# Cached attention on one core: when a load may be issued

## The chip, the cores and the metric

The kernel runs on one core of one Trainium2 chip. The metric is the device time of one execution in microseconds (us), lower is better. The profile is one execution, recorded by the hardware profiler; its span goes from the first to the last instruction.

## The reference

Two independent blocks A and B of multi-head attention with a key/value cache, each followed by an output projection; the results stand side by side in the output. All tensors are bf16, `B, Sq, D = 16, 64, 640`, `H, Sk, Dh = 32, 512, 128`.

```
def _A_ref(x, k_cache, v_cache, wq, wo):
    q = (x @ wq).reshape(B, Sq, H, Dh).transpose(0, 2, 1, 3)
    scores = jnp.einsum("bhqd,bhkd->bhqk", q, k_cache) * (Dh ** -0.5)
    p = softmax(scores, axis=-1)
    o = jnp.einsum("bhqk,bhkd->bhqd", p, v_cache)
    return o.transpose(0, 2, 1, 3).reshape(B, Sq, H * Dh) @ wo
return jnp.concatenate([A(...), B(...)], axis=-1)
```

Each block reads 2 x 67 MB of keys and values, which are used once.

## The kernel before

The work is cut into four passes (two blocks, each in two halves of 16 heads). A pass goes over 8 pairs of batches, and a pair over its 16 heads, one head of both batches at a time. Two heads make one step `m` (256 steps), and two steps make a chunk of four heads (128 chunks).

For each step TensorE transposes the keys (`em_KX`, L586), multiplies them with the queries (`em_SM`, L632), transposes the probabilities (`em_TR2`, L670), multiplies them with the values (`em_PV2`, L694), and adds the heads' outputs times `wo` (`em_OP2` and `em_OX`, L709 and L719). The projection of the queries (`em_Q`, L603) is spread between these. VectorE copies the transposed keys (L593), takes the row maxima (L641) and the reciprocals; ScalarE computes the exponentials (L647); GpSimd scales the rows (L661).

The order of every engine's instructions is fixed when the program is built: `PHASES` gives each kind of operation an offset in steps and a place in a period, `build_plan` sorts by the resulting planned time `ts`, and `prune_waits` leaves of all dependences only the semaphore waits that are not implied by others. On TensorE a wait is attached to a matmul; where an operation needs more waits than its first instruction and the last one of the operation before it can carry, a separate waiting instruction stands ahead of it.

All loads are issued by SyncE (its rows in the profile say SPq), in one order, sorted by a key: the planned time of the first use less `LEAD` or `WLEAD` steps, or, if that is later, the planned time at which the buffer comes free. A step needs one load of keys (`LDK`, 512 KB, `kn_ring`, 9 buffers) and one of values (`LDV`, 512 KB; `v_ring` has 5 buffers, each of two halves with a load of its own, and a chunk needs both halves). Loads of 640 KB bring 16 slices each of `wq` and `wo`; `x` comes in three loads (block A) and eight of 160 KB (block B, `xr_ring`). SyncE issues in program order, so a load that waits holds all loads behind it.

When a load may be issued is what the change touches. Before, the plan holds a model of TensorE's time (`STEP_US`), of the time that each load takes (`DMA_US`) and a time before which no load is counted (`START_US`). For each load it takes the modelled time `t_now`, but at the latest `BEFORE` (3.88) steps ahead of the first use, finds the TensorE operation planned for that time, and makes the load wait for it (`paced`). This comes on top of the wait for a free buffer. Both halves of a `v_ring` buffer count on one semaphore; the waiting instruction waits for both.

Of the kernel before, what the change touches and what calls it, by code (L numbers as in the profile page):

```python
# [15 lines left out]
class Cfg:  # L16
# [5 lines left out]
    NVP = 5  # L22
    LEAD = 5.37
    WLEAD = 5.48
    STEP_US = ((8, 3.68), (32, 27.17), (160, 3.12), (216, 3.1), (256, 3.43))
    DMA_US = dict(LDK=1.40, LDV=1.44, LDWQ=1.8, LDWO=1.8, LDX=0.45, LDXR=0.5)
    START_US = 210.96
    BEFORE = 3.88
    NKT = 3
    NXR = 2  # L30
    NP = 4
# [108 lines left out]
def build_plan(dims, cfg):  # L140
# [17 lines left out]
    KT = dims["KT"]  # L158
# [5 lines left out]
    progs = {e: [] for e in ENGINES}  # L164
# [21 lines left out]
    for k in range(NPER - PPQ):  # L186
        u, i, hc = k // PPQ, k % PPQ // HG, k % HG
# [20 lines left out]
    def x_of(k):  # L208
        u, b = (k - HG) // PPQ + 2, (k - HG) % PPQ // HG
        if k % HG or u < 4 or u >= NPER // PPQ or u % 4 > 1:  # L210
            return None
        return u // 4, u % 2 * QB + b
# [102 lines left out]
    for n, (k_lo, *templates) in enumerate(cfg.PHASES):  # L315
        k_hi = cfg.PHASES[n + 1][0] if n + 1 < len(cfg.PHASES) else 0
        for eng, template in zip(("pe", "act", "dve", "pool"), templates):
            for kind, off, sub, t in template:
                for m in range(2 * (k_lo % NPER) + off % 2, 2 * (k_hi % NPER or NPER), 2):
                    op = make_op(kind, m, sub, m - off + 2 * t / cfg.PERIOD)  # L320
# [11 lines left out]
    loads = []  # L332
# [5 lines left out]
    for ps_ in range(NPASS):  # L338
        for j in range(HG):
            ready = []  # L340
            if ps_:
                first = ("QN", (2 * ps_ - 1) * MPQ + j * MPG, 0)
                ready = [("QN", (2 * ps_ - 2) * MPQ + j * MPG + MPG - 2, 0)]
            else:
                first = ("QZ", 2 * j - 2, 0 if j > 1 else G) if j else ("QJ", 0, 0)
            add(ready, first, cfg.WLEAD, 0, "LDWQ", (ps_, j), [("wq", qslot(j))], (ps_, j))
            i = ps_ * HG + j
# [8 lines left out]
    for n, m in enumerate(xts):  # L356
        xb, b = x_of(m // 2)
# [8 lines left out]
            [("v", k % cfg.NVP, j)], m)  # L366


    def us(t):
        us_, a = min(t, 0) * cfg.STEP_US[0][1], 0  # L370
        for b, step in cfg.STEP_US:
            us_ += step * max(0, min(t, b) - a)
            a = b
        return us_

    pe_us = [us(op.ts) for op in progs["pe"]]
    paced = []
    t_now = cfg.START_US
    for key, first, _, op in sorted(loads, key=lambda e: e[:3]):
        t_now = max(t_now, us(key))  # L380
        i = bisect.bisect_right(pe_us, min(t_now, us(first - cfg.BEFORE))) - 1
        if i > 0:
            paced.append((op, progs["pe"][i]))
        progs["sp"].append(op)
        t_now += cfg.DMA_US[op.kind] * (op.aux[2] - op.aux[1] if op.kind == "LDX" else 1)

    counts = {}

    def sem_key(op):
        if op.kind in ("LDK", "LDV", "LDXR"):  # L390
            return ("d_" + op.kind[2:].lower(), op.writes[0][1])
        if op.kind == "LDX":
            return ("d_x", op.aux[1])
        if op.kind in ("LDWQ", "LDWO"):
            return ("d_" + op.kind[2:].lower(), op.writes[0][1])
        if op.kind == "ST":
            return ("d_out",)
        if op.kind in ("INIT1", "INIT2"):
            return ("s_init",)
        return ("s_" + op.kind.lower(),)  # L400

    def assign(op):
        key = sem_key(op)
        counts[key] = counts.get(key, 0) + 1
        op.sem = key
        op.count = counts[key]
# [11 lines left out]
    for op in sorted(all_ops, key=lambda o: (o.ts, ENGINES.index(o.eng))):  # L418
# [6 lines left out]
        for res in op.writes:  # L425
# [3 lines left out]
            for rd in readers.get(res, ()):  # L429
                if rd is not op:  # L430
# [2 lines left out]
            readers[res] = []  # L433
        op.deps = [d for d in deps if d is not op and not (d.eng == op.eng and op.eng in ("pe", "sp"))
                   and not (d.dma and op.dma and d.eng == op.eng)]
    for op, d in paced:
        op.deps.append(d)
    info = dict(NSTEP=NSTEP, NMAC=NMAC, NCHUNK=NCHUNK, NGRP=NGRP, HG=HG, NBP=NBP, SPB=SPB, NHALF=NHALF,
                NPASS=NPASS, counts=counts, KT=KT, wslot=wslot, qslot=qslot, QB=QB, PPQ=PPQ, qcell=qcell,
# [63 lines left out]
def mha_kernel(nc, blocks, out, cfg=None):  # L503
# [12 lines left out]
    N1 = DN - N0  # L516

    progs, info = build_plan(dict(NBLK=NBLK, B=B, H=H, KT=KT), cfg)
    prune_waits(progs)
    NBP, SPB, NHALF = info["NBP"], info["SPB"], info["NHALF"]  # L520
# [413 lines left out]
```

## Time and profile before

| | |
|---|---|
| median of 3 runs | 852.0 us (849.78 to 853.32) |
| the profiled execution: its own time | 852.97 us |
| its span | 851.0 us |
| mean granted TensorE clock | 0.998 |
| TensorE busy (matmul) | 811.3 us, 95% |
| VectorE, ScalarE, GpSimd busy | 727.9, 644.7, 417.1 us |
| read from HBM | 292.03 MB, of it 292.06 MB on SyncE's queue (by packets) |

The profile's page lists busy time by engine, the span in 40 slices, the DMA queues, the chain of work that ended last, groups of instructions by source line, and the DMA issues with their median time from issue to landing. "PEld" is TensorE's loading of weights. A row such as "PE ps L603 <- issue: 18.0, 113, 0.2" says that TensorE sat idle ahead of line 603 for 18.0 us in total, 113 times, at most 0.2 us, and that nothing which the profile shows was waited for. Queue q1 carries SyncE's loads, q10 the stores of the output (issued by ScalarE), q8 and q14 the engines' instructions.

### The profile page before, as it was taken

The numbers are of one execution on the slowest core, as the hardware profiler recorded it, in microseconds if no ns is written. First come the engines' busy times: TensorE is split into PE (matmuls) and PEld (weight loads), VectorE is DVE, ScalarE is ACT, GpSimd is POOL, SyncE is SP. The second block draws the span as 40 slices with busy tenths as digits, with TensorE's granted clock in tenths as the row PEclk, the third lists the DMA queues.
The fourth block names the chain that finished last, engine by engine and source line by source line (L and its number), as shares of the span: only waits on it lengthen the run. The fifth ranks groups of instructions, "written<-read, shape, count | busy, mean of one in ns | idle before, by whom it ended". The sixth has DMA issues, their size and how long they took to land.

```text
span 851.0 us, 38366 instructions
## 1 busy us (share of the span) xinstructions
PE 811.3 (95%) x17025; PEld 566.4 (67%) x17156; DVE 727.9 (86%) x1192; ACT 644.7 (76%) x1466; POOL 417.1 (49%) x518
## 2 busy tenths in 40 slices
PE   8999999999999999999999998999999999999996
PEld 5566676666666666666666666666666666666664
DVE  4688888888888898888899887988888989989994
ACT  2678877777777787777877877787887877778886
POOL 0355455454544554454554545455455455455553
PEclk9999999999999999999999999999999999999999
DMA  9999999999999999999999999999999999999992
GB/s 306 360 354 349 369 354 352 348 338 362 354 352 353 369 369 363 359 360 367 364 362 367 364 360 349 321 362 362 360 360 363 366 369 365 366 339 352 370 321 89
DMA packets 228438, 297.14 MB, mean 349 GB/s; under 512 B 9136, under 2 KB 162736, under 8 KB 228272
## 3 DMA queue, kind: packets, MB, share of 16 engines
q1 hardware_dynamic: 225968, 292.06, 100.3%
q8 instruction: 134, 2.20, 1.1%
q10 hardware_dynamic: 2304, 2.62, 0.9%
q14 instruction: 32, 0.26, 0.1%
HBM read 292.03 MB, written 2.62 MB: 346 GB/s over the span
## 4 chain that ended last, share of the span: by engine, by line
PE 89%; issue 3%; ACT 3%; DMA 2%; DVE 2%; SPq 0%; ACTq 0%
PE ps L586 17%; PE ps L694 15%; PE ps L603 15%; PE ps L632 14%; PE ps L670 13%; PE ps L709 12%; PE ps L719 3%; ACT p_ring L647 2%; DMA v_ring<-in_A_v_cache_dram 1%; DVE negmax L641 1%; ACT pT_ring L684 1%; DMA wq_sb<-in_A_wq_dram 1%; DVE ktp_ring L593 1%; PE ps L804 0%; PE ps L813 0%
## 5 line engine op out<-in xcount | busy, mean ns | idle before, releaser
L661 POOL TENSOR_SCALAR pn_ring<-p_ring,recip 128x512 bf16<-128x512 bf16 x512 | 416.4, 843 | 425.1 <-DVE recip L653 379.0
L647 ACT ACTIVATE p_ring<-ps,negmax 128x512 bf16<-128x512 f32 x512 | 349.0, 688 | 74.0 <-DVE negmax L641 68.5
L593 DVE COPY ktp_ring<-ps 128x2048 bf16<-128x2048 bf16 x256 | 312.1, 1219 | 56.3 <-PE ps L586 56.2
L641 DVE TENSOR_REDUCE negmax<-ps 128x1 f32<-128x512 f32 x512 | 328.3, 683 | 16.2 <-PE ps L632 8.5
L586 PEld LDWEIGHTS ps<-ident,kn_ring 64*128 64x128 bf16 x8192 | 136.8, 95 | 107.9 <-issue 96.4
L586 PE MATMUL ps<-ident,kn_ring 64*128 64x64 bf16 x8192 | 169.2, 191 | 3.3 <-issue 1.4
L603 PE MATMUL ps<-xT_sb,wq_sb 128*128 128x512 bf16 (+2 forms) x543 | 133.4, 372 | 19.0 <-issue 18.1
L670 PEld LDWEIGHTS ps<-ident,pn_ring 128*128 128x128 bf16 x2048 | 125.4, 98 | 38.8 <-ACT p_ring L647 7.2
L694 PE MATMUL ps<-pT_ring,v_ring 128*128 128x64 bf16 x4096 | 143.5, 194 | 2.8 <-issue 1.9
L701 ACT ACTIVATE oT_ring<-ps 128x512 bf16<-128x512 f32 x128 | 76.4, 597 | 91.7 <-PE ps L694 91.7
L684 ACT ACTIVATE pT_ring<-ps 128x1024 bf16<-128x1024 bf16 (+1 forms) x144 | 140.9, 987 | 3.0 <-DVE pT_ring L680 2.2
L670 PE MATMUL ps<-ident,pn_ring 128*128 128x128 bf16 x2048 | 138.9, 219 | 3.4 <-issue 1.6
L709 PE MATMUL ps<-wo_sb,oT_ring 128*128 128x512 bf16 x498 | 135.3, 379 | 4.0 <-issue 1.9
L632 PE MATMUL ps<-ktp_ring,qc_ring 128*64 128x512 bf16 x1024 | 135.5, 385 | 0.7 <-issue 0.7
L694 PEld LDWEIGHTS ps<-pT_ring,v_ring 128*128 128x128 bf16 x4096 | 128.2, 98 | 9.6 <-issue 2.4
L647 ACT ACTIVATION_READ_ACCUMULATOR p_ring<-ps,negmax 128x1 f32 x512 | 104.8, 205 | 0.0
L680 DVE COPY pT_ring<-ps 128x1024 bf16<-128x1024 bf16 (+1 forms) x128 | 82.5, 644 | 14.6 <-PE ps L670 14.1
L619 ACT ACTIVATE qc_ring<-ps 128x512 bf16<-128x512 f32 (+1 forms) x129 | 76.8, 596 | 21.5 <-PE ps L603 21.4
L603 PEld LDWEIGHTS ps<-xT_sb,wq_sb 128*128 128x128 bf16 x660 | 53.8, 98 | 54.0 <-issue 1.1
L632 PEld LDWEIGHTS ps<-ktp_ring,qc_ring 128*64 128x64 bf16 x1024 | 47.2, 109 | 34.1 <-issue 1.3
L709 PEld LDWEIGHTS ps<-wo_sb,oT_ring 128*128 128x128 bf16 x512 | 42.7, 98 | 25.0 <-ACT pT_ring L684 2.1
L653 DVE RECIPROCAL recip<-rowsum 128x2 f32<-128x2 f32 x256 | 39.8, 155 | 4.4 <-ACT p_ring L647 4.4
(21 smaller groups left out, 127.2 us busy)
## 6 DMA issues: line engine op xcount, KB each, us to landing
kn_ring<-in_A_k_cache_dram SPq DMA_DIRECT2D x128, 512.0 KB, 6.5
v_ring<-in_A_v_cache_dram SPq DMA_DIRECT2D x128, 512.0 KB, 6.8
kn_ring<-in_B_k_cache_dram SPq DMA_DIRECT2D x128, 512.0 KB, 6.3
v_ring<-in_B_v_cache_dram SPq DMA_DIRECT2D x128, 512.0 KB, 6.5
wq_sb<-in_A_wq_dram SPq DMA_DIRECT2D x8, 640.0 KB, 7.1
wo_sb<-in_A_wo_dram SPq DMA_DIRECT2D x8, 640.0 KB, 7.2
wq_sb<-in_B_wq_dram SPq DMA_DIRECT2D x8, 640.0 KB, 6.8
wo_sb<-in_B_wo_dram SPq DMA_DIRECT2D x8, 640.0 KB, 6.6
```

Of the source, the lines that this page charges most:

```text
L586: last = e.transpose(kt_ps[hs][:, 64 * t:64 * t + 64], kn_ring[r, m % NKB, t // 8, t % 8 * DH:(t % 8 + 1) * DH], ident[r, r])
L593: ins = e.tensor_copy(ktp_ring[:, ktslot(op.idx)], ps[:, b:b + 2, :].rearrange("p b s -> p (b s)").bitcast(BF16))
L603: last = e.matmul(dst[:, col:col + n], wq_sb[:, qslot(hh // G), kt, (hh % G) * DH:(hh % G + 1) * DH], xT_sb[:, kt, lo * 128:hi * 128], sta ...
L632: ins = e.matmul(s_bank(g)[64 * j:64 * j + 64, :], q[:, 64 * j:64 * j + 64], kt[:, sub, j], start=True, stop=True, tile_position=(0, 64 * j))
L641: ins = e.reduce_max(negmax[:, r:r + 1], s_bank(g), axis=AX.X, negate=True)
L647: ins = e.activation(p_ring[:, g % NP, :], s_bank(g), ACTF.Exp, bias=negmax[:, r:r + 1], scale=1.0, accum_out=rowsum[:, r:r + 1])
L661: ins = e.tensor_scalar(dst, src, recip[:, r:r + 1], 1.0, ALU.mult, ALU.mult)
L670: ins = e.transpose(pt_flat(m)[:, (4 * sub + t) * 128:(4 * sub + t + 1) * 128], pn_ring[:, g % NPN, t * 128:(t + 1) * 128], ident[:, :])
L680: ins = e.tensor_copy(*pt_copy(op.idx, op.aux))
L684: ins = e.activation(*pt_copy(op.idx, op.aux), ACTF.Copy)
L694: ins = e.matmul(qo_ps[:, col:col + 64], v_ring[:, m // 2 % NVP, j, 2 * (m % 2) + sub, t * DH:(t + 1) * DH], pT_ring[:, m % NT, sub, t, 64 ...
L709: ins = e.matmul(out_ps, oT_ring[:, m // 2 % NO, 2 * (m % 2) + sub, :], wo_sb[:, wslot(ps_, hh // G), hh % G, 0:N0], start=(hh == 0), stop ...
```

## The change

The models of time and the waits for TensorE's operations go. SyncE's order of loads stays. A load now waits for its buffer, and for the landing of earlier loads, so that it and all loads not known to have landed come to at most `CAP` = 1,750,000 bytes. For loads of keys and values alone that is three at a time (1,572,864 bytes); two of these and one of weights (1,703,936 bytes) fit as well. Since loads are now waited for one by one, each half of a `v_ring` buffer gets a semaphore of its own.

```diff
-    STEP_US = ((8, 3.68), (32, 27.17), (160, 3.12), (216, 3.1), (256, 3.43))
-    DMA_US = dict(LDK=1.40, LDV=1.44, LDWQ=1.8, LDWO=1.8, LDX=0.45, LDXR=0.5)
-    START_US = 210.96
-    BEFORE = 3.88
+    CAP = 1750000
...
-    for key, first, _, op in sorted(loads, key=lambda e: e[:3]):
-        t_now = max(t_now, us(key))
-        i = bisect.bisect_right(pe_us, min(t_now, us(first - cfg.BEFORE))) - 1
-        if i > 0:
-            paced.append((op, progs["pe"][i]))
-        progs["sp"].append(op)
-        t_now += cfg.DMA_US[op.kind] * (op.aux[2] - op.aux[1] if op.kind == "LDX" else 1)
+    def size(op):
+        if op.kind in ("LDK", "LDV"):
+            return 1 << 19
+        if op.kind in ("LDWQ", "LDWO"):
+            return KT << 17
+        return (KT << 15) * (op.aux[2] - op.aux[1] if op.kind == "LDX" else 1)
+
+    progs["sp"] = [l[3] for l in sorted(loads, key=lambda e: e[:3])]
+    capped = []
+    moved, under_way = 0, 0
+    for op in progs["sp"]:
+        under_way += size(op)
+        while under_way > cfg.CAP:
+            under_way -= size(progs["sp"][moved])
+            moved += 1
+        if moved:
+            capped.append((op, progs["sp"][moved - 1]))
...
-        if op.kind in ("LDK", "LDV", "LDXR"):
+        if op.kind == "LDV":
+            return ("d_v",) + op.writes[0][1:]
+        if op.kind in ("LDK", "LDXR"):
...
-    for op, d in paced:
+    for op, d in capped:
         op.deps.append(d)
```

In the built program every engine's operations stand in the same order as before. On SyncE the waits differ. On TensorE 115 separate waiting instructions are new, all ahead of `em_PV2` (L694), 112 of them because the two halves of the values now have two semaphores.

More of the change, by code (lines that the diff above doesn't have):

```diff
@@ L366, in build_plan @@
             [("v", k % cfg.NVP, j)], m)
[L369 to L378, printed above, removed]
-    for key, first, _, op in sorted(loads, key=lambda e: e[:3]):
-        t_now = max(t_now, us(key))
-        i = bisect.bisect_right(pe_us, min(t_now, us(first - cfg.BEFORE))) - 1
-        if i > 0:
-            paced.append((op, progs["pe"][i]))
-        progs["sp"].append(op)
-        t_now += cfg.DMA_US[op.kind] * (op.aux[2] - op.aux[1] if op.kind == "LDX" else 1)
+    def size(op):
[14 more added lines that the diff above has]
+            capped.append((op, progs["sp"][moved - 1]))
     counts = {}
     def sem_key(op):
-        if op.kind in ("LDK", "LDV", "LDXR"):
+        if op.kind == "LDV":
+            return ("d_v",) + op.writes[0][1:]
+        if op.kind in ("LDK", "LDXR"):
             return ("d_" + op.kind[2:].lower(), op.writes[0][1])
```

## The prediction

> **What bounds the kernel now.** I read the page first: busy time by engine and the chain of work that ended last.
>
> ```profile
> span 851.0 us, 38366 instructions
> ...
> PE 811.3 (95%) x17025; PEld 566.4 (67%) x17156; DVE 727.9 (86%) x1192; ACT 644.7 (76%) x1466; POOL 417.1 (49%) x518
> ...
> PE 89%; issue 3%; ACT 3%; DMA 2%; DVE 2%; SPq 0%; ACTq 0%
> ```
>
> TensorE is busy for 95% of the span and carries 89% of the chain; DMA carries 2%. Then the waits of TensorE from 36 us to the end, thirteen rows, of which these are the first three and the last:
>
> ```profile
> PE ps L603 <- issue: 18.0, 113, 0.2
> PE ps L709 <- issue: 1.9, 12, 0.2
> PE ps L694 <- issue: 1.9, 3, 1.1
> ...
> PE ps L586 <- ACT pT_ring L684: 0.5, 3, 0.2
> ```
>
> None of the thirteen names a DMA. Once the kernel has started, no matmul waits for a load, so a load that comes earlier is worth nothing there. Third, the DMA view, for the stretch from 100 to 800 us:
>
> ```profile
> GB/s 368 343 356 344 340 357 355 355 352 351 371 367 368 362 357 368 359 364 360 366 368 366 362 359 317 340 363 358 359 365 361 361 367 369 361 371 364 333 356 365
> DMA packets 192412, 250.73 MB, mean 358 GB/s; under 512 B 7720, under 2 KB 136249, under 8 KB 192270
> ## 3 DMA queue, kind: packets, MB, share of 16 engines
> q1 hardware_dynamic: 190398, 246.51, 102.7%
> ...
> kn_ring<-in_B_k_cache_dram SPq DMA_DIRECT2D x122, 512.0 KB, 6.2
> v_ring<-in_B_v_cache_dram SPq DMA_DIRECT2D x115, 512.0 KB, 6.5
> v_ring<-in_A_v_cache_dram SPq DMA_DIRECT2D x103, 512.0 KB, 6.7
> kn_ring<-in_A_k_cache_dram SPq DMA_DIRECT2D x97, 512.0 KB, 6.5
> ```
>
> The packets on q1 fill the 16 DMA engines all the time, and TensorE consumes 358 GB/s of at most 371 that a slice shows (slices are 17.5 us): four per cent of room. So TensorE sets the time, with the stream of loads close behind it. The last column is the point: a load lands 6.2 to 6.7 us after its issue. At 358 GB/s and 6.5 us some 2.33 MB are under way, between four and five loads. The change allows 1.75 MB.
>
> **The change part by part.** *The waits for TensorE go.* SyncE's waits show what they cost now:
>
> ```profile
> SPq L792 <- PE ps L632: 103.6, 74, 2.9
> SPq L792 <- PE ps L709: 78.5, 73, 2.6
> SPq L792 <- PE ps L603: 73.1, 29, 4.2
> ```
>
> These are hundreds of microseconds on SyncE's queue, but behind a waiting load stand only other loads, and no matmul waits for those. Their end is worth nothing after the start. What comes late next is the load's buffer (every second load of keys still waits for the transposes nine steps before it, L586) or the landing of earlier loads.
>
> *The wait for landings comes.* With loads of 524,288 bytes, three are under way; the fourth is issued when the first has landed, and everything behind it on SyncE's queue, weights and `x` included, waits too. If the stream never pauses for a buffer, it goes in rounds: each round moves three loads (1.573 MB), and takes as long as a load needs from issue to landing with two others ahead of it. TensorE's pace of 358 GB/s needs a round of at most 1.573 MB / 358 GB/s = 4.39 us. Two bounds from below. At the best rate, 371 GB/s, a round takes 4.24 us. And a load alone takes, by the first load of the program and by the last of the values:
>
> ```profile
> kn_ring<-in_A_k_cache_dram SPq DMA_DIRECT2D x1, 512.0 KB, 3.9
> ...
> v_ring<-in_B_v_cache_dram SPq DMA_DIRECT2D x1, 512.0 KB, 3.9
> ```
>
> So three under way just cover the latency: 3.9 against 4.24, a margin of 0.34 us, and the room to 4.39 is 0.15 us. What disturbs a round is the fetching of instructions, on the same 16 engines. The page has it for the whole span:
>
> ```profile
> q1 hardware_dynamic: 225968, 292.06, 100.3%
> q8 instruction: 134, 2.20, 1.1%
> ```
>
> 134 packets of 16.4 KB each hold one of the 16 engines, and a load has landed only when its part on every engine has. My reasoning, which no row shows yet: with four or five loads queued, an engine that was held still has work queued and the others go on; with three, the next issue waits for the slowest engine, and the others run dry. The price of one packet, from above: 1.1% x 16 x 851 us / 134 = 1.12 us by the packets' own time, less the margin of 0.34, is 0.78 us. From below: 16.4 KB at a sixteenth of 371 GB/s is 0.71 us, less 0.34, is 0.37 us. (Zero, where the engine was ahead anyway, is the first rival.) I take 0.5 us, nearer to the lower end, because the packet's own time also holds data packets that went between. Fewer bytes in the queue speed nothing up that TensorE waits for, so I see no gain here.
>
> In 1.573 MB rounds, 292.06 MB are 186 rounds: 186 x 4.24 = 789 us undisturbed, and 134 x 0.5 = 67 us of disturbance (50 to 105). Together that is 856 us, or 341 GB/s, less than the 358 that TensorE takes: the stream becomes the bound.
>
> Here the Trainium skill speaks the other way. "DMA: Bandwidth & Descriptors", section "Anatomy of one DMA", gives a DMA's time as a fixed 2.0 us and its bytes at 436 GB/s, which would be 3.2 us for 512 KB; the rows here have 3.9 for a load alone. By the page's figure the margin would be about 1.0 us and would take up nearly all of a packet's 1.12: the sum would come out near 790 us for the stream, and TensorE would stay the bound, as in the first rival. The page fitted loads issued by GpSimd, these are SyncE's, and the measured row decides.
>
> *The start.* The order of loads is the same, and the first load is issued at 0.8 us as now. The chain between 0 and 34 us shows the loads setting the time already:
>
> ```profile
> 1.77 5.60 DMA wq_sb<-in_A_wq_dram
> ...
> 21.92 11.65 DMA v_ring<-in_A_v_cache_dram
> ```
>
> The rounds of the start are in the 186, so they need no term of their own.
>
> *The end.* The last values are issued at 834.9 us and land 3.9 us later, 12.3 us before the end; the matmuls that use them start at 844.8 in the chain, some 6 us before it.
>
> ```profile
> L789 SPq DMA_DIRECT2D v_ring<-in_B_v_cache_dram x128: 367/368/1122, 436.3 to 834.9; - x128
> ...
> 844.84 0.95 PE ps L694 x32
> ```
>
> After the last landing there remain 6 to 12 us; I take 9.
>
> *115 more waits on TensorE.* The landing they ask for is nearly always there when TensorE keeps waiting for the younger half anyway. Behind each stand all later matmuls, and ScalarE's copy of the outputs waits for them. No separate wait shows in this trace. Nearest from below: ahead of L694, where a wait is attached to the first matmul of every pair today, there are 1.9 us of unexplained idle time in all, so about zero. From above: L603 loses 18.0 us in 113 places, 0.16 us each, or 18 us for 115. I take 3 us, near the row of the same line. While the stream is the bound, they are hidden in TensorE's new idle time; if that cover is gone, they are paid.
>
> *The sum*, against the profiled execution's 852.97 us (span 851.0, and 2.0 around it; the median of three is 852.0): 0.8 + 789 + 67 + 9 + 2 = 868 us. With the bounds of the packet's price and of the end it is 848 to 908; below about 853 TensorE would set the time.
>
> **The rivals.** *Three loads are enough.* The engines that fall behind are not the slowest ones, a packet costs close to nothing, and the stream of 789 us runs ahead of TensorE until the buffers are full; then a load waits for the transposes nine steps before it, and TensorE paces the loads as now. For it: the lone landing of 3.9 is below 4.24, and the buffers allow more lead than 3.88 to 5.37 steps. Against it: 0.15 us of room per round. Time: 853 plus the 115 waits, 856 (853 to 871).
>
> *The start gets shorter*, the case of a faster kernel. SyncE's queue has this wait in the first 36 us:
>
> ```profile
> SPq L792 <- PE ps L813: 4.9, 2, 4.3
> ```
>
> An early load of keys is held for TensorE's transposes of `x`. If that hold falls away whole, all that follows at the start comes 4.9 us sooner, and if the stream then keeps TensorE's pace, the kernel takes 848 us. Against it: the same load now waits for the landing of the third load, issued at 1.77 and landed 5.60 us later, at 7.4, about when the hold ended. It decides only if that landing comes earlier by microseconds.
>
> **How the numbers follow.** The stream as bound gets 0.62, at 868 us; three loads being enough 0.30, at 856; the shorter start 0.08, at 848. A measurement of this kernel can tell about 0.5% from no change. Of the first rival two thirds stay within that (0.20), one third is slower by more (0.10), which with the 0.62 makes 0.72 slower, and 0.08 faster. The range of 847 to 900 takes in both rivals and leaves out the dearest part of the main case, where each packet costs over 0.7 us.
>
> **What would show it.** In the changed kernel's DMA view, landing falls from 6.2 to 6.7 to some 4.3 to 4.8 us, and the stretch from 100 to 800 us runs at about 341 GB/s. TensorE's waits name `kn_ring` and `v_ring` loads, and its chain has DMA at well over 2%. SyncE waits for DMA queues, hardly ever for L586. I am wrong if TensorE's waits still name no DMA after the start and SyncE waits for L586: then three loads suffice. If landing is at 5 us or more, the price per round is larger than any row here told.

## The result, and the profile after

The changed kernel takes 1000.5 us (median; 996.4 the fastest), the kernel before 852.0: 1.174 times as long, 95% interval 1.170 to 1.177. I had forecast 868, within 847 to 900. One of the five executions of the changed kernel took 1580 us, for a reason that nothing on record shows, and the ratio leaves it out. The direction and the place were right, the size was wrong by a factor of nine.

The page of the kernel after, busy time, queue and chain:

```profile
span 994.5 us, 38607 instructions
...
PE 847.5 (85%) x17025; PEld 583.3 (59%) x17156; DVE 730.8 (73%) x1192; ACT 647.7 (65%) x1466; POOL 417.4 (42%) x518
...
q1 hardware_dynamic: 225968, 292.06, 89.5%
...
DMA 92%; PE 6%; ACT 1%; issue 1%; DVE 0%; SPq 0%; ACTq 0%
```

The chain has turned over: 92% DMA where it was 2%. And yet the DMA engines are less busy than before, 89.5% where it was 100.3%. The bound is a stream whose engines are not always busy: a load is held back by the landing of an earlier one. The DMA view from 100 to 800 us:

```profile
GB/s 320 304 300 318 307 269 290 303 303 308 301 279 318 300 324 316 322 290 310 316 303 305 318 305 313 319 300 296 310 312 300 288 305 298 296 314 302 277 270 295
...
q1 hardware_dynamic: 161928, 209.12, 90.7%
...
v_ring<-in_A_v_cache_dram SPq DMA_DIRECT2D x109, 512.0 KB, 5.2
kn_ring<-in_A_k_cache_dram SPq DMA_DIRECT2D x102, 512.0 KB, 5.3
```

Landing fell from about 6.5 to 5.2 us, as fewer loads queue, but not to the 4.3 to 4.8 that the forecast named; over 5 us was its sign that a round costs more than any row of before told. 209.12 MB in 700 us are 299 GB/s, or 5.27 us for a round of three loads (1.573 MB). How a round looks on SyncE's queue:

```profile
600.56 0.37 SPq L789 DMA_DIRECT2D v_ring<-in_B_v_cache_dram  x1
602.13 0.37 SPq L792 DMA_DIRECT2D kn_ring<-in_B_k_cache_dram  x1
604.33 0.37 SPq L789 DMA_DIRECT2D v_ring<-in_B_v_cache_dram  x1
605.62 0.37 SPq L792 DMA_DIRECT2D kn_ring<-in_B_k_cache_dram  x1
```

Every issue follows the landing of the load three before it, so from 600.56 to 605.62, three issues on, is one round, 5.06 us. TensorE's waits, and SyncE's:

```profile
PE ps L694 <- DMA v_ring<-in_B_v_cache_dram: 59.5, 42, 5.0
PE ps L694 <- DMA v_ring<-in_A_v_cache_dram: 53.1, 34, 5.0
```

```profile
SPq L789 <- DMA kn_ring<-in_B_k_cache_dram: 146.0, 110, 3.5
SPq L789 <- DMA kn_ring<-in_A_k_cache_dram: 128.2, 97, 3.0
...
SPq L792 <- PE ps L586: 2.0, 7, 0.4
```

The values come late (L694, 112.6 us), and SyncE waits for landings and hardly ever for a buffer (L586, 2.0 us): the loads hardly ever run ahead as far as the buffers allow. TensorE's busy time is 36 us longer as well, 847.5 where it was 811.3, at a granted clock of 0.954 (0.998 before). With 92% of the chain on DMA I take this as time that the loads set anyway; no run tests it alone.

### The profile page after: what moved, and what is told of

Read it like the earlier page. It is cut to its first block, busy times and chain, and to the rows that moved or that the text cites. A ratio compares the mean times of both kernels' runs of the same rounds, so it can differ in the third digit from the quotient of the medians.

```text
span 994.5 us, 38607 instructions
## 1 busy us (share of the span) xinstructions
PE 847.5 (85%) x17025; PEld 583.3 (59%) x17156; DVE 730.8 (73%) x1192; ACT 647.7 (65%) x1466; POOL 417.4 (42%) x518
## 3 DMA queue, kind: packets, MB, share of 16 engines
q1 hardware_dynamic: 225968, 292.06, 89.5%
## 4 chain that ended last, share of the span: by engine, by line
DMA 92%; PE 6%; ACT 1%; issue 1%; DVE 0%; SPq 0%; ACTq 0%
DMA v_ring<-in_B_v_cache_dram 22%; DMA kn_ring<-in_B_k_cache_dram 22%; DMA v_ring<-in_A_v_cache_dram 21%; DMA kn_ring<-in_A_k_cache_dram 20%; DMA wq_sb<-in_B_wq_dram 2%; PE ps L694 2%; DMA wo_sb<-in_B_wo_dram 2%; PE ps L632 2%; DMA wq_sb<-in_A_wq_dram 1%; PE ps L586 1%; DMA outp<-in_A_x_dram 1%; DMA wo_sb<-in_A_wo_dram 1%; PE ps L709 1%; ACT p_ring L647 0%; PE ps L603 0%
## 5 line engine op out<-in xcount | busy, mean ns | idle before, releaser
L694 PE MATMUL ps<-pT_ring,v_ring 128*128 128x64 bf16 x4096 | 151.5, 198 | 113.6 <-DMA v_ring<-in_B_v_cache_dram 59.5
L694 PEld LDWEIGHTS ps<-pT_ring,v_ring 128*128 128x128 bf16 x4096 | 136.1, 101 | 125.7 <-DMA v_ring<-in_B_v_cache_dram 64.3
L586 PEld LDWEIGHTS ps<-ident,kn_ring 64*128 64x128 bf16 x8192 | 140.9, 97 | 111.7 <-issue 104.0
L586 PE MATMUL ps<-ident,kn_ring 64*128 64x64 bf16 x8192 | 172.7, 194 | 1.3 <-ACT pT_ring L684 1.0
L603 PE MATMUL ps<-xT_sb,wq_sb 128*128 128x512 bf16 (+2 forms) x543 | 135.6, 376 | 20.6 <-issue 19.8
L632 PE MATMUL ps<-ktp_ring,qc_ring 128*64 128x512 bf16 x1024 | 152.5, 424 | 0.0
L603 PEld LDWEIGHTS ps<-xT_sb,wq_sb 128*128 128x128 bf16 x660 | 54.7, 99 | 57.3 <-issue 6.5
L632 PEld LDWEIGHTS ps<-ktp_ring,qc_ring 128*64 128x64 bf16 x1024 | 50.7, 117 | 39.7 <-issue 10.5
L709 PEld LDWEIGHTS ps<-wo_sb,oT_ring 128*128 128x128 bf16 x512 | 42.7, 98 | 25.7 <-ACT pT_ring L684 2.1
```

The costliest lines, as they stand in the source:

```text
L586: last = e.transpose(kt_ps[hs][:, 64 * t:64 * t + 64], kn_ring[r, m % NKB, t // 8, t % 8 * DH:(t % 8 + 1) * DH], ident[r, r])
L603: last = e.matmul(dst[:, col:col + n], wq_sb[:, qslot(hh // G), kt, (hh % G) * DH:(hh % G + 1) * DH], xT_sb[:, kt, lo * 128:hi * 128], sta ...
L632: ins = e.matmul(s_bank(g)[64 * j:64 * j + 64, :], q[:, 64 * j:64 * j + 64], kt[:, sub, j], start=True, stop=True, tile_position=(0, 64 * j))
L694: ins = e.matmul(qo_ps[:, col:col + 64], v_ring[:, m // 2 % NVP, j, 2 * (m % 2) + sub, t * DH:(t + 1) * DH], pT_ring[:, m % NT, sub, t, 64 ...
L709: ins = e.matmul(out_ps, oT_ring[:, m // 2 % NO, 2 * (m % 2) + sub, :], wo_sb[:, wslot(ps_, hh // G), hh % G, 0:N0], start=(hh == 0), stop ...
```

## The experiments

The theories. A: too few bytes are under way; a round waits for a load's whole way there and back. B: the loss of the pacing by TensorE costs by itself. C: the 115 further waits on TensorE cost. My forecast's own reason, that the fetching of instructions disturbs the rounds, is tested against A from s1_stream3 on. Theory D came later, out of the result without a limit: a queue that is too deep holds up the fetching of instructions.

**One load more under way** (e1_cap4):

```diff
-    CAP = 1750000
+    CAP = 2100000
```

> Theory A, too few bytes under way: a round of loads lasts as long as the slowest of 16 engines needs, 5.3 us with three loads in it, and the engines run dry meanwhile. With CAP 2,100,000 four loads of 512 KB are under way; if landing stays at about 5.6 to 5.9 us, 4 x 0.524 MB / 5.8 us is 362 GB/s, as fast as TensorE takes them: 855 to 880 us. Rival B, the loss of the pacing by TensorE is what costs (order of landing and use, bursts): four under way changes little, 960 us or more.

902.6 us, 1.059 times the kernel before (1.052 to 1.066). One load more gives back 98 of the 148 us, which is for A. It isn't the 855 to 880 that I expected: L694 still waits for values, 45.5 us in all.

**No limit** (e2_nocap): `CAP = 1 << 30`, so that loads wait for their buffers alone.

> No limit on the bytes under way, loads wait for their buffers alone. Theory A: TensorE is the bound again, no load is late, 853 to 862 us with the 115 extra waits on TensorE. Rival B: still far above 870 us, because the loads are not tied to TensorE. A queue as deep as the buffers allow would show landing at 10 us or more.

888.5 us, 1.040 times (1.034 to 1.045). Neither theory: most of the loss is gone, but 36 us stay. TensorE's waits in this kernel:

```profile
PE ps L586 <- issue: 13.2, 25, 1.6
...
PE ps L670 <- issue: 6.5, 11, 1.3
PE ps L694 <- issue: 5.1, 15, 0.9
PE ps L603 <- issue: 4.5, 6, 1.4
```

After the start no row names a load. What grew is "issue", idle time in which nothing that the profile shows was waited for, in pieces of up to 1.6 us. All "issue" rows of TensorE come to about 33 us. In the kernel before they were 26.5, of which 18.0 at L603 were no idle time: there 543 of 660 matmuls of that line are recorded, and in runs with all 660 the row of 0.16 us pieces is absent. That leaves 8.5 us, and in e3_twosem (below), the kernel before with all matmuls recorded, it is 3.9. The queue is deeper than before, in bursts, since SyncE now waits for the buffer of nearly every second load of keys and then issues what stood behind; a load lands after some 8 us, not the 10 or more of my expectation:

```profile
SPq L792 <- PE ps L586: 395.4, 112, 7.2
```

```profile
kn_ring<-in_A_k_cache_dram SPq DMA_DIRECT2D x128, 512.0 KB, 7.6
v_ring<-in_A_v_cache_dram SPq DMA_DIRECT2D x128, 512.0 KB, 8.7
```

**The two semaphores alone** (e3_twosem): the kernel before with

```diff
-        if op.kind in ("LDK", "LDV", "LDXR"):
+        if op.kind == "LDV":
+            return ("d_v",) + op.writes[0][1:]
+        if op.kind in ("LDK", "LDXR"):
```

> The kernel before with only the semaphores of the values split in two halves, and so with the extra waits on TensorE. My term was 3 us of 0 to 18: 852 to 856 us. Rival C, that the extra waiting instructions stop TensorE's queue: 860 us or more.

853.4 us beside 852.4, ratio 1.0008 (0.9984 to 1.0031). The trace of this kernel has 128 separate waiting instructions on TensorE more than before, so it covers the 115 of the change. C is out; these waits cost at most 2.6 us.

**Pacing and limit together** (e4_paced_cap3): the kernel before, with the limit of 1.75 MB added to the pacing and the two semaphores.

> Before's pacing by TensorE's operations and the limit of 1.75 MB together. Theory A: the limit alone costs it all, about 1000 us, because a load that is late at its landing makes the paced operation late too; at least 985. Rival B: the pacing keeps the stream regular, below 900 us.

1004.3 us, ratio 1.177 (1.171 to 1.183). The limit alone makes the whole loss, whether loads are paced or not. B is out for the change as made.

**The stream by itself** (s1_stream3): all computing left out, and with it the waits for buffers; the loads keep their order and limit, and zeros are stored at the end. This kernel and the four others whose names begin with s were run once each.

```diff
+    progs["pe"], progs["dve"] = [], []
...
+    progs["act"] = [mk("act", "ZERO", -1, [("ident",)], [("out_sb", "V"), ("out_sb", "X")], 10000)]
```

> Only the loads, in the changed kernel's order and with its limit of three loads, and at the end sixteen stores of zeros: all computing is left out, so hardly any instructions are fetched. As I predicted (disturbance by fetched instructions is the price): rounds of 4.24 to 4.4 us, some 360 to 371 GB/s, landing 4.2 us, about 800 to 825 us in all. Theory A (the slowest of 16 engines and the way there and back are the price, with or without other work): rounds near 5.0 us, 315 GB/s, about 940 us.

958.0 us. This is the run that finds the error. The DMA view of this kernel from 100 to 800 us:

```profile
q1 hardware_dynamic: 168048, 217.15, 93.5%
q14 instruction: 4, 0.03, 0.0%
...
v_ring<-in_A_v_cache_dram SPq DMA_DIRECT2D x108, 512.0 KB, 5.1
```

Four packets of instructions in 700 us, and still 310 GB/s, 5.07 us per round. No other work disturbs this stream, and still the engines are idle for some of the time.

**The stream beside matmuls that fetch instructions** (s2_stream3_pe): as before, and 17,000 matmuls on a constant.

> The same stream beside 17,000 matmuls on TensorE that read a constant, so that instructions are fetched at the full kernel's rate; the rest of the computing is left out. If fetched instructions are the price: landing goes from 4.2 to 5.2 us and the stream from 370 to about 300 GB/s between the first and this run. If they cost little: landing within 0.3 us of the run without them.

From 100 to 600 us, while TensorE works:

```profile
q1 hardware_dynamic: 116813, 150.97, 91.2%
q8 instruction: 95, 1.56, 1.2%
...
v_ring<-in_A_v_cache_dram SPq DMA_DIRECT2D x109, 512.0 KB, 5.3
```

302 GB/s, 5.21 us per round: about one packet per round (95 in 96 rounds) costs 0.14 us. I had put 0.5, with 0.37 as the lower bound. The term on which I built the loss is nearly nothing, and the one that I took as undisturbed is nearly all.

**Smaller steps** (s3_stream6half): the stream alone, 1.75 MB, each load of keys and values cut in two.

> The same stream and the same limit of 1.75 MB, with each load of keys and values cut into two of 256 KB, six under way; computing left out. If bytes under way alone set the rate: the same rate as with three loads of 512 KB. If the size of the step counts (the next issue waits for a whole load on its slowest engine): 5 to 12 percent faster, because 1.31 to 1.57 MB stay under way where it was 1.05 to 1.57.

**Four under way** (s4_stream4): the stream alone with `CAP = 2100000`.

> The same stream with four loads under way (CAP 2,100,000), computing left out. Theory A: rounds of four in 5.7 to 6.0 us, 350 to 368 GB/s. If three were enough without the other work: no faster than with three, 371 GB/s in both.

864.3 and 850.5 us beside 958.0. Here are the two from 100 to 800 us, first the cut loads, then the four:

```profile
q1 hardware_dynamic: 193934, 242.24, 102.0%
...
kn_ring<-in_B_k_cache_dram SPq DMA_DIRECT2D x230, 256.0 KB, 4.3
```

```profile
q1 hardware_dynamic: 190131, 246.14, 103.5%
...
kn_ring<-in_B_k_cache_dram SPq DMA_DIRECT2D x120, 512.0 KB, 5.7
```

346 and 352 GB/s, with full engines. At the same limit, six pieces of 256 KB move 12% more than three of 512 KB: with a coarse step one third of the queue is refilled at once, and only when the last of its 16 parts has landed. In the trace's semaphore events the 16 parts of a load land within 0.5 us of each other in the first load of the program, and within 1.5 us (median) in the stream of three. That the engines which finish first then stand idle fits the 93.5%. But the spread is 1.4 us with four under way too, where the engines are full, and no run takes it away, so this part is argued.

**Cut loads in the whole kernel**, six and nine under way (e5_half6, e6_half9): the keys' buffers are two resources and the values' four, each with its load and semaphore; TensorE waits for all of them.

```diff
-            return 1 << 19
+            return 1 << 18
...
+        for h in range(2):
+            add(..., "LDK", (m, h), [("kn", m % cfg.NKB, h)], (m, h))
```

> The changed kernel with the same limit of 1.75 MB, each load of keys and values cut into two of 256 KB with a semaphore of its own. Theory A, with the size of the step: the stream alone ran at 342 GB/s so cut (308 uncut), instruction fetches take some per cent off: 865 to 895 us instead of 1000. If only the bytes under way counted: 990 us or more. If the further waits on TensorE (two per step for the keys, up to four per chunk for the values) cost: above 900.

> The same cut with CAP 2,400,000, nine loads of 256 KB, about the bytes that before's pacing kept under way. Theory A and D (a deep queue holds up the fetching of instructions, which is what no limit at all lost): enough for TensorE and not deeper than before, 850 to 868 us, few stalls of TensorE at block borders. If the loss of the pacing costs in another way: 880 us or more, like no limit.

Six: 947.9 us, ratio 1.116 (1.112 to 1.121): better than 1000 at the same limit, and far from the 865 to 895 that the stream alone had promised; from 100 to 800 us 346 GB/s became 315 beside the other work. Nine: 860.5 us, ratio 1.014 (1.013 to 1.016). This kernel has no pacing either. Its loads run ahead until a buffer is missing, though less than with no limit: SyncE waits 51.3 us for the transposes (here L588), where it was 395.4. It loses 11 us where no limit lost 36. Its waits of TensorE:

```profile
PE ps L588 <- issue: 6.9, 9, 1.4
PE ps L696 <- issue: 2.7, 8, 0.4
...
PE ps L815 <- DMA wq_sb<-in_A_wq_dram: 1.8, 1, 1.8
```

**Six whole loads** (e7_cap6): `CAP = 3200000`.

> The changed kernel with CAP 3,200,000, six whole loads under way. Theory D: no load is late, TensorE stalls on its instructions a little less than with no limit (888 us) and more than before: 868 to 888 us. If the queue's depth does not matter to instructions: 853 to 860 us.

886.6 us (876.8 to 890.3), ratio 1.041 (1.034 to 1.047), at the upper end of D's range and not to be told from no limit (888.5).

**Instruction fetch against a deep queue** (s5_stream8_pe): the matmuls on a constant beside a stream with `CAP = 4300000`.

> The loads with eight under way (CAP 4,300,000) beside 17,000 matmuls on a constant; the rest of the computing is left out. TensorE here waits for nothing but its instructions, every 128 matmuls: with three loads under way it sat idle 158 us in 116 places, 1.4 us each. Theory D: a deeper queue makes each of these longer, by 1 to 4 us, 280 to 600 us in all. If depth does not matter to the instruction queue (it has a ring of its own): within 20% of 158 us.

TensorE's only wait after the start, with eight loads under way, and then in s2_stream3_pe, with three:

```profile
PE ps L845 <- issue: 260.6, 125, 2.6
```

```profile
PE ps L845 <- issue: 158.1, 116, 2.9
```

and the shape of it in time, in the deep one, in the middle and at the end:

```profile
310.05 3.89 PE L845 MATMUL ps<-ones_sb,ident 128*128 128x64 bf16 x128 [1.03 <-issue]
...
814.54 26.90 PE L845 MATMUL ps<-ones_sb,ident 128*128 128x64 bf16 x905 [1.05 <-issue]
```

These matmuls depend on no load and no other engine, and stop every 128: 2.1 us each with eight loads under way (364 GB/s), 1.4 us with three (302 GB/s). Depth, or the fuller stream that goes with it, makes each stop 0.7 us longer, less than the 1 to 4 us that I had expected. The last load lands at 811.9 us, and the 905 matmuls after that run without a stop.

The trace also has every packet of instructions (q8). All 123 stops with eight loads, after the first 36 us, end 1.2 to 1.7 us after the end of such a packet. So do 33 of TensorE's 38 pauses of over 0.4 us in the kernel without a limit (25.7 of 30.0 us) and 25 of 31 with six whole loads; a moment picked at random would do so in 7 or 8 of 100 cases. In e3_twosem there are 8 such pauses in all, 3 of them with this mark. This ties most of the pauses in the kernels with a deep queue to the fetching of instructions. From one packet's end to the next it is 6.47 us (median, during the matmuls) with eight loads and 5.28 with three, and the kernel before goes from block to block in 6.2 us. By this estimate, fetching beside eight loads is no faster than TensorE's own pace.

The Trainium skill, "Runtime: NRT & Kernel Launch", section "Instruction fetch mechanics", says that an engine refills its instructions in blocks of 256 through a DMA queue of its own, and that crossing a block is mostly hidden. The trace agrees on the block, 128 matmuls with their 128 weight loads, and not on the hiding while loads run; without them, over the 905 matmuls, it was hidden. These matmuls use up a block in 3.9 us, faster than the whole kernel does.

**The price of the cutting, and ten under way** (e8_paced_half: before's pacing, loads cut; e9_half10: `CAP = 2650000`):

> The pacing of the kernel before, no limit, with each load of keys and values cut in two of 256 KB and a semaphore for each. Theory D: with the pacing the queue is no deeper than before, so cut loads change nothing and the further waits on TensorE are nearly free: 848 to 856 us; the cut kernel with nine under way then loses its 1.4% by its limit or its buffers. If the cutting itself (twice the loads, more waits on TensorE) is what that kernel lost: 858 us or more.

> The cut loads with ten under way (CAP 2,650,000) in place of nine. Theory A and D: between too shallow (948 us at six) and too deep (889 with no limit) the curve is flat near nine; one more makes the stream safer and the fetching of instructions slower: 856 to 868 us. If nine was still too shallow: below 855; if depth counts more than I think: above 868.

853.5 us, ratio 1.0039 (1.0007 to 1.0071): cutting costs 0 to 0.7%, so it is at most a part of the 1.3 to 1.6% that nine under way lost. Ten under way take 866.8 us, ratio 1.017 (1.013 to 1.022). Of six, nine and ten, nine is the best; no version beat the kernel before.

## Why the prediction was right and wrong

**TensorE's bound and the useless lead: right.** After the start no matmul waited for a load before, and freeing the loads from TensorE bought nothing. **The stream becomes the bound: right**, with landing waits on SyncE in place of TensorE's, and L694 waiting.

**"186 x 4.24 = 789 us undisturbed": this is the step that failed.** The undisturbed round is 5.07 us (s1_stream3), 943 us for 186. The 0.83 us more in each round are 154 us, where the whole forecast was 132 us short. I took the larger of two lower bounds, 371 GB/s and a lone landing of 3.9 us, as the value itself. Both were measured where the bound did not bite: the 371 with more than four loads queued, the 3.9 with none ahead. A round of three loads is neither of these but a closed loop of its own, and no row of before showed its time. I had no upper end for it, which made the range too short. That three under way are too few is shown, by the loads alone with three and four; why a round takes 5.07 and not 4.24 us stays open.

**The packet's price, 0.5 us (0.37 to 0.78): wrong, 0.14 us** between s1 and s2, below the lower bound. 134 x 0.14 is 19 us where I had 67. With 5.27 us as measured in the kernel, which includes this, 186 rounds are 980 us; with my 0.8, 9 and 2 us around them it is 992, and 996 to 1002 were measured. The frame of the sum was right, its main term was not.

**115 waits, 3 us of 0 to 18: right in size** (1.0 us for 128 of them in e3_twosem, -1.4 to 2.6 by the interval), but the upper bound, L603's 18.0 us, was no idle time: those matmuls were missing from the trace.

**The rival "three loads are enough"** rested on 3.9 being below 4.24, which is the same error; so did the sum by the Trainium skill's "DMA: Bandwidth & Descriptors", section "Anatomy of one DMA". Its figure gives 3.2 us for 512 KB; the lone load here took 3.9, and one with two others under way 5.1. **The shorter start** did not come: the first values were used at 37.5 us where it was 33.7.

**"Fewer bytes in the queue speed nothing up that TensorE waits for": only half right.** It holds for the change, which starves the stream. But a deep queue also reaches TensorE, by its instructions. Between the profiled runs of e3_twosem and e2_nocap, which have the same matmuls recorded, the span grew by 38.7 us: TensorE's issue idle by 29 us, most of it behind instruction packets, and its busy time by 8.7 us (833.0 to 841.7), for which I have no reason. Depth was not separated from the fullness of the stream or its bursts. That the pacing gains by this alone isn't shown: nine cut loads come within 1.4% without it.

## What to carry to other kernels

A limit on the bytes under way is a closed loop: measure its rate with the loads alone before taking the stream's best rate and a lone load's latency for it. Here three loads of 512 KB gave 310 GB/s, four 352, and six of 256 KB, the same bytes, 346. A deep queue cost as well: with six whole loads or no limit, 36 us or so, with TensorE's pauses mostly behind the fetching of instructions. Pacing the issue by the consumer kept some 2.3 MB under way and paid neither price.

## What the hardware showed that I had not expected

- Beside a stream of loads, TensorE stops at blocks of 256 instructions: 1.4 us per block with three loads of 512 KB under way, 2.1 us with eight, in matmuls that depend on no load. Once the loads had landed, 905 matmuls ran without a stop.
- The same limited stream ran at 346 GB/s alone and at 315 beside the other work when cut in six, at 352 and 326 with four whole loads, but at 310 and 299 with three (all from 100 to 800 us). What of the other work takes this was not separated.
- Separate waiting instructions ahead of matmuls, 128 of them in e3_twosem, could not be told from none (0.9984 to 1.0031).
